# Converting w_in on a timetable during attention, with v loaded from ScalarE's queue and half of the transposed tiles copied by VectorE

## The chip, the cores and the metric

The kernel runs on one core of one Trainium2 chip. A core has five engines that work side by side, each through its own instructions in order: TensorE (PE, matmuls and transposes; PEld is its weight load), VectorE (DVE), ScalarE (ACT), GpSimd (POOL) and SyncE (SP), which here only starts transfers (DMA) between HBM and the on-chip memory. An instruction that waits for a semaphore holds back everything behind it on its engine. The metric is the device time of one execution in microseconds (us); three runs of the kernel before gave a median of 913.17 us (910.35 to 913.26).

## The reference

Three stages follow each other. Inputs are float32 for q, k and v; the five weight matrices are float64 (a float32 array times a NumPy float64 scalar).

```
q, k, v: (4 batches, 8 heads, 576 positions, 64)
scores = q @ k^T / 8
  heads 0-3: row i sees columns i-31..i            ("local")
  heads 4-7: row i sees columns j<=i, j%32 == i%32 ("strided")
attn = softmax(scores) @ v       -> x: 2304 tokens x 512
h = x @ w_in (512 x 2048);  x = (h * cos(h)) @ w_out (2048 x 512)
g = x @ w_gate; val = x @ w_val (512 x 1536 each)
out = (silu(g) * val) @ w_out2 (1536 x 512)
```

## The kernel before

**Three stretches.** Attention comes first, then the first pair of matrices (w_in, w_out) for five blocks of tokens, then the gated pair. Each wide product is made of three float16 matmuls (`mm3`, L502): the float32 number is scaled and split into a high float16 part, written by ScalarE (`hi_part`), and a low part, written by VectorE (`lo_part`). The scale needs the largest magnitude of the whole matrix, so a matrix is read in full before its first product.

**Attention in steps.** One run is one batch with its four local or its four strided heads; there are eight runs, alternating, and each run has three groups (`Duo`), so 24 groups. The loop at L675 goes through steps k = 0 to 29. Step k issues the mask and score matmuls of group k, the row maxima of group k (`tops`, VectorE, then GpSimd), the exponentials of group k-1 (ScalarE), the sums (VectorE) and the normalisation (GpSimd) of group k-2, the transposes of group k-3 (TensorE) and their copies from the matmul memory (`evac`, L442: two per group, both ScalarE), the product with v of group k-4, and the copy of the result of group k-5 into the token array (`put`, ScalarE). A run uses its q and k from step 3i on and its v from step 3i+4 on. Steps 24 to 29 only drain the pipeline; step 25 also issues the first product with w_in (`up1`, L694), in TensorE's queue ahead of the v products of that step.

**Loads.** All loads are issued by SyncE in the order of the program: q and k of a run (`load_qk`, three buffers), v of a run (`load_v`, two buffers of each kind), and raw float64 weights (`load_raw`, L155, 1 MB per pair of tiles, three buffers; the next pair is issued when the conversion of the oldest has been emitted). w_in has eight raw pairs, w_out comes behind it.

**Conversions.** A raw pair of w_in becomes float32 in four pieces (`conv_steps`, L202): g0 on ScalarE waits for the load and makes a first float32 form, g1 on VectorE takes the maxima of the raw pair, g2 and g3 on VectorE add the low bits. These pieces stand in one list (`fill`), with all the work on weights that follows. `pump(share)` is called twice per step: it adds the share to a credit and emits pieces from the list while the credit is above 0, and every piece takes its cost from the credit. `need(key)` emits pieces until the named one is out, whatever the credit says. Before, the whole list stands there from the start, `pump` begins at step KP = 4, and `begin` puts g0 of a pair ahead of g1 to g3 of the pair before it. In the list the scale and split of the first token block stand between w_in's pairs, and behind the pairs come the maximum of w_in, one scan of w_out, w_in's scale, its split into parts, and the other scans of w_out.

**First matrix pair.** Slots of the loop at L894 are one `up1` each (twelve matmuls); from slot HEAD = 16 on, `down1` (the product with w_out) is issued too, which needs w_out's parts tile by tile. SHARE, SHARE2 and HSHARE say how much VectorE work on later weights each slot emits.

## Time and profile before

| | us |
|---|---|
| median of three runs | 913.17 |
| profiled execution, device time | 910.2 |
| its span, first to last instruction | 908.2 |
| PE busy | 859.4 (95%) |
| DVE busy | 599.1 (66%) |
| ACT busy | 489.0 (54%) |
| POOL busy | 179.0 (20%) |
| mean granted TensorE clock | 0.979 of full speed |

The rows stand in a section below. In a row of a timeline the first two numbers are the start and the length in us, then engine, source line, operation, tiles and shapes; the bracket says how long the engine had stood idle and what ended the wait. A busy share is an average over the three stretches, so the attention stretch (up to about 110 us) has to be read by itself.

### The profile page before, as it was taken

The numbers are of one execution on the slowest core, as the hardware profiler recorded it, in microseconds if no ns is written. First come the engines' busy times: TensorE is split into PE (matmuls) and PEld (weight loads), VectorE is DVE, ScalarE is ACT, GpSimd is POOL, SyncE is SP. The second block draws the span as 40 slices with busy tenths as digits, with TensorE's granted clock in tenths as the row PEclk, the third lists the DMA queues.
The fourth block names the chain that finished last, engine by engine and source line by source line (L and its number), as shares of the span: only waits on it lengthen the run. The fifth ranks groups of instructions, "written<-read, shape, count | busy, mean of one in ns | idle before, by whom it ended". The sixth has DMA issues, their size and how long they took to land.

```text
span 908.2 us, 16426 instructions
## 1 busy us (share of the span) xinstructions
PE 859.4 (95%) x6687; PEld 564.6 (62%) x6687; DVE 599.1 (66%) x1038; ACT 489.0 (54%) x942; POOL 179.0 (20%) x202
## 2 busy tenths in 40 slices
PE   8578988998999989999999999999999999999997
PEld 5457744443444434455656677777767777888885
DVE  5358879998578879885778455555644555564544
ACT  4469878864446657554667443443434443444433
POOL 4134404311134546622222100000000000000000
PEclk9689999999999999999999999999999999999999
DMA  9977525257545545553141442424425343544500
GB/s 281 302 257 248 187 114 212 93 186 297 212 183 182 204 151 197 200 209 137 47 174 68 176 163 82 163 109 182 148 97 183 114 156 128 200 183 185 200 1 35
DMA packets 24642, 150.90 MB, mean 166 GB/s; under 512 B 3016, under 2 KB 4296, under 8 KB 11640
## 3 DMA queue, kind: packets, MB, share of 16 engines
q1 hardware_dynamic: 24568, 149.87, 46.3%
q8 instruction: 52, 0.85, 0.4%
q14 instruction: 22, 0.18, 0.1%
HBM read 134.13 MB, written 15.73 MB: 165 GB/s over the span
## 4 chain that ended last, share of the span: by engine, by line
PE 78%; DVE 7%; DMA 6%; ACT 5%; POOL 2%; issue 2%; SPq 0%; POOLq 0%; DVEq 0%; ACTq 0%
PE bank L503 14%; PE bank L504 14%; PE bank L505 14%; PE acc L504 11%; PE acc L505 11%; PE acc L503 11%; DMA raw<-w_in 3%; DMA vs<-v_s 2%; DVE tb L539 1%; PE sc L405 1%; DVE cv L241 1%; PE bank L439 1%; ACT arena L253 1%; DVE arena L256 1%; POOL arena L551 1%
## 5 line engine op out<-in xcount | busy, mean ns | idle before, releaser
L503 PE MATMUL bank<-xs,wi 128*128 128x256 f16 (+3 forms) x744 | 224.9, 302 | 10.9 <-DVE q L134 9.1
L504 PE MATMUL bank<-xs,wi 128*128 128x256 f16 (+3 forms) x744 | 225.0, 302 | 0.0
L505 PE MATMUL bank<-xs,wi 128*128 128x256 f16 (+3 forms) x744 | 224.6, 302 | 0.0
L503 PE MATMUL acc<-arena 128*128 128x512 f16 (+1 forms) x560 | 200.4, 358 | 1.0 <-ACT arena L625 1.0
L504 PE MATMUL acc<-arena 128*128 128x512 f16 (+1 forms) x560 | 200.4, 358 | 0.3 <-DVE arena L626 0.3
L505 PE MATMUL acc<-arena 128*128 128x512 f16 (+1 forms) x560 | 200.4, 358 | 0.0
L551 POOL TENSOR_TENSOR arena<-tb,arena 128x512 f16<-128x512 f32 (+1 forms) x80 | 90.3, 1130 | 248.5 <-ACT arena L550 231.6
L962 DVE TENSOR_TENSOR arena<-bank,cv 128x512 f32<-128x512 f32 (+1 forms) x90 | 57.1, 635 | 117.6 <-PE bank L505 117.6
L505 PEld LDWEIGHTS <-arena 128*128 128x128 f16 x952 | 93.1, 98 | 57.1 <-issue 0.5
L504 PEld LDWEIGHTS <-arena 128*128 128x128 f16 x952 | 93.2, 98 | 53.4 <-issue 1.5
L503 PEld LDWEIGHTS <-arena 128*128 128x128 f16 x952 | 93.2, 98 | 52.6 <-issue 0.6
L504 PEld LDWEIGHTS <-wi 128*128 128x128 f16 x768 | 75.5, 98 | 50.7 <-issue 14.1
L503 PEld LDWEIGHTS <-wi 128*128 128x128 f16 x768 | 75.6, 98 | 43.7 <-issue 6.5
L504 PE MATMUL bank<-xs,arena 128*128 128x256 f16 (+1 forms) x392 | 102.4, 261 | 0.0
L503 PE MATMUL bank<-xs,arena 128*128 128x256 f16 (+1 forms) x392 | 102.4, 261 | 0.0
L505 PE MATMUL bank<-xs,arena 128*128 128x256 f16 (+1 forms) x392 | 102.4, 261 | 0.0
L505 PEld LDWEIGHTS <-wi 128*128 128x128 f16 x768 | 75.5, 98 | 35.4 <-issue 2.4
L625 ACT ACTIVATE arena<-tb 128x512 f16<-128x512 f32 (+1 forms) x60 | 35.2, 587 | 111.0 <-DVE tb L621 111.0
L536 ACT ACTIVATE tb<-bank,quarter,c 128x512 int32<-128x512 f32 (+1 forms) x74 | 53.6, 724 | 47.7 <-PE bank L505 41.8
L614 ACT ACTIVATE tb<-arena,c 128x512 f32<-128x512 f32 (+1 forms) x60 | 40.7, 679 | 66.4 <-DVE arena L962 65.4
L550 ACT ACTIVATE arena<-tb 128x512 f16<-128x512 f32 (+1 forms) x80 | 46.6, 582 | 42.7 <-PE acc L505 38.4
L620 DVE SCALAR_TENSOR_TENSOR tb<-tb,arena 128x512 f32<-128x512 f32 (+1 forms) x60 | 38.0, 634 | 38.9 <-ACT tb L614 38.9
(120 smaller groups left out, 1206.9 us busy)
## 6 DMA issues: line engine op xcount, KB each, us to landing
raw<-w_out SPq DMA_DIRECT2D x28, 1024.0 KB, 4.9
wi<-w SPq DMA_DIRECT2D x16, 1792.0 KB, 7.5
arena<-w SPq DMA_DIRECT2D x14, 1792.0 KB, 7.4
raw<-w_gate SPq DMA_DIRECT2D x12, 1024.0 KB, 4.9
raw<-w_val SPq DMA_DIRECT2D x12, 1024.0 KB, 5.2
w<-arena SPq DMA_DIRECT2D x42, 256.0 KB, 2.1
raw<-w_in SPq DMA_DIRECT2D x8, 1024.0 KB, 20.2
qk<-qk_s SPq DMA_DIRECT2D x4, 1188.0 KB, 7.6
```

The lines of the kernel that those rows point to most:

```text
L241: nc.vector.scalar_tensor_tensor(out=u, in0=box["l"], scalar=29, in1=u, op0=ALU.logical_shift_right, op1=ALU.bitwise_or)
L253: nc.scalar.activation(out=dst, in_=src, func=AF.Copy, scale=s)
L503: nc.tensor.matmul(out=o, lhsT=w[:, 0, c], rhs=x[0], start=first, stop=False, **kw)
L504: nc.tensor.matmul(out=o, lhsT=w[:, 0, c], rhs=x[1], start=False, stop=False, **kw)
L505: nc.tensor.matmul(out=o, lhsT=w[:, 1, c], rhs=x[0], start=False, stop=last, **kw)
L536: nc.scalar.activation(out=c["w"].bitcast(I32), in_=c["ph"], func=AF.Identity, scale=turn[c["blk"]], bias=quarter)
L550: nc.scalar.activation(out=g[:, 0, 0:n], in_=w, func=AF.Copy)
L551: nc.gpsimd.tensor_tensor(out=g[:, 1, 0:n], in0=w, in1=g[:, 0, 0:n], op=ALU.subtract)
L614: nc.scalar.activation(out=t, in_=c["C"][m][:, 0, 0:n], func=AF.Tanh, scale=half[c["blk"]])
L620: nc.vector.scalar_tensor_tensor(out=t, in0=t, scalar=1.0, in1=gate, op0=ALU.add, op1=ALU.mult)
L625: nc.scalar.activation(out=g[:, 0, 0:n], in_=t, func=AF.Copy)
L962: nc.vector.tensor_tensor(out=c["C"][m][:, :, h * right:h * right + h], in0=p, in1=t, op=ALU.add)
```

## The change

Five things are edited. (1) The pairs of w_in leave the common list: pair j is put in at step 4 + 3j (CONV0), g0 to g3 of a pair together; the scale and the split of the first token block are put in at steps 12 and 14; everything behind w_in's pairs is put in at step 25, when the last pair is. `pump` runs from step 0 with share 1.0, and g1 costs 1.2 where it cost 1.6. (2) In `evac` the second of a group's two tiles is copied by VectorE. (3) `load_v` is issued by ScalarE, and the loads of the second run's v and the first raw pair change places. (4) HEAD is 17 where it was 16. (5) SHARE and SHARE2 are 0.95 and 0.75 where they were 0.93 and 0.68.

```diff
--- before.py
+++ after.py
@@ -49,16 +49,16 @@
 
 LAGS = (2, 3, 4, 5)
 WARM = 11
-PUMP, KP, PACE, TAIL = 0.9, 4, 1.6, 1.2
-XSAT = 8
+PUMP, PACE, TAIL, CONV0 = 1.0, 1.2, 1.2, 4
+XSAT = 12
 EARLY, K0 = 1, 1
-HEAD, HSHARE = 16, 0.85
+HEAD, HSHARE = 17, 0.85
 RATE, MINLAG = 0.4, 2
 RAW = 3
 XM = 5
 HOMES, LATE, UNIT = 24, 4, 16
 W7S = 4
-SHARE, SHARE2, SB = 0.93, 0.68, 2
+SHARE, SHARE2, SB = 0.95, 0.75, 2
 
 
 WHERE = [((q, c), (3 + q, c)) if q < 3 else ((6, 0), (6, 256))
@@ -366,11 +366,11 @@
             b, loc = runs[i]
             if loc:
                 v_t[i] = ap.tile([LW, 2, LT, 128], F32, name="vl")
-                nc.sync.dma_start(out=v_t[i], in_=v_l[b])
+                nc.scalar.dma_start(out=v_t[i], in_=v_l[b])
             else:
                 v_t[i] = v_pads[i // 2 % 2]
                 for r in range(2):
-                    nc.sync.dma_start(out=v_t[i][64 * r:64 * r + SW, r], in_=v_s[b, r])
+                    nc.scalar.dma_start(out=v_t[i][64 * r:64 * r + SW, r], in_=v_s[b, r])
 
         def bank():
             return pm.tile([128, 512], F32, name="bank")
@@ -442,8 +442,8 @@
             def evac(self):
                 pt = ap.tile([128, 768], F32, name="pt", bufs=2)
                 self.pt = pt[0:self.rows, 0:2 * self.cols].rearrange("p (u n) -> p u n", u=2)
-                for u in range(2):
-                    nc.scalar.activation(out=self.pt[:, u], in_=self.tp[u], func=AF.Copy)
+                nc.scalar.activation(out=self.pt[:, 0], in_=self.tp[0], func=AF.Copy)
+                nc.vector.tensor_copy(out=self.pt[:, 1], in_=self.tp[1])
 
             def values(self):
                 qn, r = (64, LW) if self.loc else (SW, 64 + SW)
@@ -645,8 +645,8 @@
             nc.sync.dma_start(out=t, in_=a)
         load_qk(1)
         load_v(0)
+        load_v(1)
         load_raw()
-        load_v(1)
         load_qk(2)
         load_raw()
         load_v(2)
@@ -654,17 +654,26 @@
         warm = score_banks()[:, 0]
         for _ in range(WARM):
             nc.tensor.matmul(out=warm, lhsT=ones16, rhs=hot, start=True, stop=True)
-        for j in range(0, M1, 2):
-            chain_later(j)
-            for cost, fn in list(scale_pieces(0, sx)) if j == XSAT else list(split_pieces(0, sx, xs)) if j == XSAT + 2 else ():
-                later(cost, fn)
-        top_later("in")
-        scan_later("out", 0)
-        scale_later("in", TW_IN)
-        split_chain([("in", j, wi) for j in range(M1)], 2)
-        for j in range(1, M1 // 2):
-            scan_later("out", j)
-        top_later("out")
+        due = {CONV0 + 3 * j: [(j,)] for j in range(M1 // 2)}
+        due.setdefault(XSAT, []).append(scale_pieces(0, sx))
+        due.setdefault(XSAT + 2, []).append(split_pieces(0, sx, xs))
+
+        def work_due(k):
+            for what in due.pop(k, ()):
+                if type(what) is tuple:
+                    chain_later(2 * what[0])
+                    begin([])
+                else:
+                    for cost, fn in what:
+                        later(cost, fn)
+            if not due and k == max(XSAT + 2, CONV0 + 3 * (M1 // 2 - 1)):
+                top_later("in")
+                scan_later("out", 0)
+                scale_later("in", TW_IN)
+                split_chain([("in", j, wi) for j in range(M1)], 2)
+                for j in range(1, M1 // 2):
+                    scan_later("out", j)
+                top_later("out")
 
         steps = deque()
 
@@ -677,7 +686,8 @@
                 return gs[k - lag] if 0 <= k - lag < len(gs) else None
 
             i, g = k // 3, k % 3
-            share = 0 if k < KP else PUMP if duo(0) else TAIL
+            share = PUMP if duo(0) else TAIL
+            work_due(k)
             if duo(LAGS[3]):
                 duo(LAGS[3]).put()
             if duo(LAGS[0]):
```

ScalarE's queue around the first two conversions. The steps are 3 to 6; L230 is g0 of a pair, L446 (L445 in the change) the copy of a transposed tile, L419 the exponentials, L467 `put`. Before:

```order
L446 ACTIVATE pt<-bank 96x384 x2
L419 ACTIVATE e_s_97<-sc,mx 128x54 x8
L230 ACTIVATE wi<-raw 128x1024 x2
L467 ACTIVATE xy<-bank 128x2x192
L446 ACTIVATE pt<-bank 96x384 x2
L419 ACTIVATE e_s_98<-sc,mx 128x54 x8
L230 ACTIVATE wi<-raw 128x1024
L467 ACTIVATE xy<-bank 128x2x192
```

With the change:

```order
L373 DMA xs<-v_s 54x1536 x2
L445 ACTIVATE pt<-bank 96x384
L419 ACTIVATE e_s_97<-sc,mx 128x54 x8
L230 ACTIVATE wi<-raw 128x1024
L467 ACTIVATE xy<-bank 128x2x192
L445 ACTIVATE pt<-bank 96x384
L419 ACTIVATE e_s_98<-sc,mx 128x54 x8
L467 ACTIVATE xy<-bank 128x2x192
L445 ACTIVATE pt<-bank 128x256
```

Before, two raw pairs are asked for in step 4 and a third in step 5; now one is asked for in step 4 and none in steps 5 and 6. One L445 per group is left, and loads of v (L373) stand between the copies.

VectorE's queue from step 23 to the first split tile of w_in (the first L256): L233, L237 and L241 are g1, g2 and g3 of the last raw pair, L117 to L127 the maximum of w_in, L176 the scan of w_out, L134 to L111 the scale. Before:

```order
L237 TENSOR_SCALAR wi<-wi 128x1024
L411 TENSOR_REDUCE mx<-sc 128x8
L241 SCALAR_TENSOR_TENSOR wi<-raw,wi 128x1024
L427 TENSOR_REDUCE ls<-e_s_97 128x8
L428 RECIPROCAL ls<-ls 128x8
L117 TENSOR_REDUCE m<-pw_in 128x1
L120 TENSOR_SCALAR a<-m 128x1
L122 SCALAR_TENSOR_TENSOR p<-m,a 128x1
L127 TENSOR_SCALAR tops<-id_72,p 128x128
L411 TENSOR_REDUCE mx<-sc 128x2x3
L176 TENSOR_REDUCE pw_out<-raw 128x2
```

With the change:

```order
L427 TENSOR_REDUCE ls<-e_s_97 128x6
L428 RECIPROCAL ls<-ls 128x6
L233 TENSOR_REDUCE pw_in<-raw 128x2
L237 TENSOR_SCALAR wi<-wi 128x1024
L241 SCALAR_TENSOR_TENSOR wi<-raw,wi 128x1024
L117 TENSOR_REDUCE m<-pw_in 128x1
L120 TENSOR_SCALAR a<-m 128x1
L122 SCALAR_TENSOR_TENSOR p<-m,a 128x1
L127 TENSOR_SCALAR tops<-id_72,p 128x128
L176 TENSOR_REDUCE pw_out<-raw 128x2
L134 TENSOR_REDUCE q<-bank 128x1
L109 RECIPROCAL s_1576<-q 128x1
```

Before, the last pair's g2 and g3 stand in steps 22 and 23 between the maxima of the last groups and the maximum of w_in stands in step 24; now the last pair and all that follows stand behind the sums of the last group, in step 25.

SyncE's queue at the start: L362 loads q and k, L162 a raw pair, L369 and L373 v. Before:

```order
L362 DMA qk<-qk_s 128x2376
L369 DMA vl<-v_l 96x2304
L162 DMA raw<-w_in 128x2048
L373 DMA vs<-v_s 54x1536 x2
L362 DMA qk<-qk_l 128x2368
L162 DMA raw<-w_in 128x2048
L369 DMA vl<-v_l 96x2304
L162 DMA raw<-w_in 128x2048
```

With the change:

```order
L362 DMA qk<-qk_s 128x2376
L162 DMA raw<-w_in 128x2048
L362 DMA qk<-qk_l 128x2368
L162 DMA raw<-w_in 128x2048 x2
L362 DMA qk<-qk_s 128x2376
```

The loads of v are gone from this queue; the first four of them stand at the head of ScalarE's queue, ahead of its first table load.

## Rows read from the trace of the kernel before

**Rows 1.** Page, chain that ended last: shares by line.

```profile
PE bank L503 14%; PE bank L504 14%; PE bank L505 14%; PE acc L504 11%; PE acc L505 11%; PE acc L503 11%; DMA raw<-w_in 3%; DMA vs<-v_s 2%; DVE tb L539 1%; PE sc L405 1%; DVE cv L241 1%; PE bank L439 1%; ACT arena L253 1%; DVE arena L256 1%;
```

**Rows 2.** Waits, 0 to 260 us: waiter, line, releaser: us, times, longest.

```profile
ACT wi L230 <- DMA raw<-w_in: 23.2, 4, 11.2
```

**Rows 3.** Timeline of ScalarE and SyncE: second pair asked for; its load.

```profile
7.25 0.43 SPq L162 DMA_DIRECT2D raw<-w_in  x1
...
31.25 1.14 ACT L230 ACTIVATE wi<-raw 128x1024 f32<-128x1024 f32 x1 [11.21 <-DMA raw<-w_in]
```

**Rows 4.** Windows: stretch, busy by engine, clock, DMA share, GB/s.

```profile
0.00:50.00 50.00, 31.74 (x445) 23.80 (x445) 22.70 (x36) 19.83 (x64) 15.52 (x33) 0.83 0.98 299
...
20.00:30.00 10.00, 2.20 (x52) 1.76 (x49) 2.91 (x5) 0.04 (x1) 1.88 (x2) 0.71 1.00 300
30.00:40.00 10.00, 5.98 (x58) 4.85 (x59) 3.39 (x5) 6.34 (x20) 1.49 (x2) 0.50 1.01 333
...
90.00:100.00 10.00, 9.95 (x208) 8.65 (x204) 9.39 (x15) 9.71 (x31) 5.71 (x6) 1.00 0.42 128
110.00:120.00 10.00, 7.54 (x85) 4.50 (x83) 5.64 (x11) 7.49 (x15) 1.17 (x1) 0.84 0.20 82
```

**Rows 5.** Loads, 0 to 130 us: times issued, KB each, median us to landing.

```profile
raw<-w_in SPq DMA_DIRECT2D x8, 1024.0 KB, 20.2
...
qk<-qk_s SPq DMA_DIRECT2D x4, 1188.0 KB, 7.6
qk<-qk_l SPq DMA_DIRECT2D x4, 1184.0 KB, 19.3
vl<-v_l SPq DMA_DIRECT2D x4, 864.0 KB, 17.2
vs<-v_s SPq DMA_DIRECT2D x4, 324.0 KB
xs<-v_s SPq DMA_DIRECT2D x4, 324.0 KB
```

**Rows 6.** Timeline: TensorE at steps 21, 23, 25 and the first w_in product.

```profile
97.97 1.14 PE L405 MATMUL sc<-qk 64*64 64x54 f32 x32
...
104.26 0.91 PE L405 MATMUL sc<-qk 64*64 64x54 f32 x24
...
109.69 1.11 PE L439 MATMUL bank<-id,e_s 128*128 128x128 f32 x4 [1.92 <-POOL e_s L431]
...
110.60 0.63 PE L503 MATMUL bank<-xs,wi 128*128 128x512 f16 x1
```

**Rows 7.** Lines, 0 to 260 us: shapes, count | busy, mean ns | idle before.

```profile
L446 ACT ACTIVATE pt<-bank 96x384 f32<-96x384 f32 (+1 forms) x48 | 19.0, 459 | 2.5 <-PE bank L439 2.3
L411 DVE TENSOR_REDUCE mx<-sc 128x6 f32<-128x576 f32 (+2 forms) x24 | 15.8, 660 | 14.2 <-PE sc L405 12.6 <-POOL e_l L431 1.4
L233 DVE TENSOR_REDUCE pw_in<-raw 128x2 f32<-128x1024 f32 x8 | 9.5, 1194 | 8.2 <-DMA raw<-w_in 8.2
L241 DVE SCALAR_TENSOR_TENSOR wi<-raw,wi 128x1024 int32<-128x1024 int32 x8 | 9.5, 1193 | 0.0
L427 DVE TENSOR_REDUCE ls<-e_l 128x6 f32<-128x582 f32 x12 | 9.0, 751 | 6.2 <-ACT e_l L419 6.2
L237 DVE TENSOR_SCALAR wi<-wi 128x1024 int32<-128x1024 int32 x8 | 6.0, 746 | 0.9 <-ACT wi L230 0.9
L517 DVE TENSOR_SCALAR xy<-acc,c 128x512 f32<-128x512 f32 x2 | 1.5, 750 | 8.7 <-PE acc L505 8.7
```

**Rows 8.** Timeline of VectorE: maximum of w_in, scan, first split tile.

```profile
105.17 0.84 DVE L122 SCALAR_TENSOR_TENSOR p<-m,a 128x1 int32<-128x1 int32 x1
...
106.62 1.21 DVE L176 TENSOR_REDUCE pw_out<-raw 128x2 f32<-128x1024 f32 x1
```

**Rows 9.** Waits of TensorE, 110 to 340 us.

```profile
PE bank L503 <- DVE q L134: 6.9, 4, 3.5
PE bank L133 <- DVE tops L127: 2.5, 1, 2.5
```

## Prediction

> **What bounds the kernel now.** I read the chain of waits first. By line its long shares are the matmuls of the two later stretches, and behind them stand two loads, raw<-w_in with 3% and vs<-v_s with 2% [rows 1]: the only part of the chain that is not arithmetic lies in attention. The list of waits puts a number on it: ScalarE stood 23.2 us, in four waits, in front of g0 of a raw pair of w_in [rows 2]. The timeline shows the worst: the pair's load was issued at 7.25 and g0 began at 31.25, after 11.21 us of idling [rows 3]; the order shows that this g0 stood in step 4, in front of `put`, the copies and the exponentials of step 5, so attention stopped with it. In that stretch TensorE was busy 2.20 of 10 us and the granted clock fell to 0.71, then 0.50 [rows 4]. Last I read the windows for what is short there: from 0 to 50 us the DMA engines were busy for 0.98 of the time at 299 GB/s, between 90 and 100 only 0.42, and there TensorE was busy 9.95 of 10 us, VectorE 9.39 and ScalarE 9.71 [rows 4]. So early attention is short of bytes and spends it on weights that nobody needs yet, and late attention has every engine full.
>
> **The stall goes; what is late next.** With a pair at steps 4, 7, 10 the waits of 23.2 us lose their cause, but the bytes remain. Up to step 21 all q and k, all v but the last, and seven of eight raw pairs must have landed; the last v lies among them in the queues. That is 4 x (1188 + 1184) + 4 x 864 + 8 x 324 + 7 x 1024 = 22,704 KB [rows 5], 23.25 MB, and at 299 GB/s [rows 4] 78 us; with the start and the landing I put the scores of step 21 at 80. Before they began at 97.97 [rows 6]. Bounds: at the best 10 us of the trace, 333 GB/s [rows 4], 70 us of loading, and then the engines decide (below); at the slow end the engines' pace is worse than before.
>
> The order of the loads follows the need: the first three v no longer stand in SyncE's queue, where q and k of the third run and the raw pairs were behind them. ScalarE pays for it. It issues twelve loads, and four of them stand ahead of its first table load; the waits among them are for loads that the first scores need as well. From step 6 on a load of v waits for the v products of the same step, and the next thing on ScalarE, `put` of the next step, waits for the same products, so only a g0 or exponentials queued behind would feel it. Two queues share the start: q and k of the first run compete with v, some 2 us on the first scores, which the byte count above already holds.
>
> With one queue the DMA engines were busy for 0.98 of the first 50 us [rows 4], so I give the second queue no bandwidth. The Trainium skill says the same in "DMA: Bandwidth & Descriptors", section "Issuing engines are not separate DMA queues": transfers started by different engines run on the same DMA engines, interleave, and save only issue time. By that rule the 78 us stand; if ScalarE's queue had bandwidth of its own, SyncE's would carry 16,656 KB, an estimated 57 us, and the engines would decide alone.
>
> **The engines' pace.** Steps 21 to 23 took (104.26 - 97.97) / 2 = 3.15 us each [rows 6]. ScalarE loses one copy per group, 24 x 0.459 = 11 us [rows 7], and gains twelve load issues. VectorE gains 24 copies. The trace has no such copy on VectorE: the nearest row from the same memory is 750 ns for 512 columns (L517), the lower end is ScalarE's 459 ns for 384 or 256; scaled by columns L517 gives 0.56 and 0.38, and I take 0.47 [rows 7]. Per three steps VectorE then has 3 x (0.66 maxima + about 0.85 sums and reciprocal + 0.47) = 5.9, and one pair 1.19 + 0.75 + 1.19 = 3.1 [rows 7], together 9.0 or 3.0 per step, beside TensorE's 3.15. That fits on average. But the pair now falls into one step: about 5.1 us of VectorE in a step of 3.15, which then has two steps to catch up. Between 0 and 0.6 us per step; I take nearly 0, since the bytes hold the steps back anyway.
>
> **Step 25.** From step 21's scores to the transposes of step 25 it was 109.69 - 97.97 = 11.7 us [rows 6]; 80 + 11.7 = 91.7. There the cost of the timetable comes due: the last pair and all behind it stand in step 25, ahead of the first product. On VectorE in a row: sums 0.75, the pair 3.1 [rows 7], the maximum of w_in 106.62 - 105.17 = 1.45, and from the scan to the first product 110.60 - 106.62 = 4.0 with other work between [rows 6, 8]; 9.3 at most, and without that other work 8.4. The first product with w_in comes at about 100 where it came at 110.6: a gain of 10.6 us. TensorE has little to do in these 8 us, since the v products of step 25 stand behind the first product.
>
> **After attention.** Both matrix stretches keep TensorE busy nearly throughout, so the gain should carry to the end, less three things. The forced pieces leave a debt in the credit, so scans and conversions of w_out are emitted later by several slots, and in the order the maximum, scale and first split of w_out now stand directly before the first `down1`, where three slots lay between. One more slot (HEAD) covers part. Priced by the same chain, 4.0 us, against 2.5 that TensorE waited for such a maximum before [rows 8, 9]: I take +2, from -2.5 to +6. The idle gap in step 25 drops the clock: it was 0.84 from 110 to 120 after a short gap [rows 4]; +1, from 0 to 3. SHARE and SHARE2 emit later weights sooner; the last blocks have room on VectorE, so 0, and if VectorE fills there the waits for its scale (6.9 us in four [rows 9]) grow by some of themselves, 0 to 4.
>
> **Sum.** -10.6 + 2 + 1 = -7.6. The profiled execution took 910.2 (span 908.2 and 2.0 around it), so 902.6. It was the fastest of the times seen, 3 below the median of 913.2; for a median I add half of that: 904.
>
> **Rivals.** *Loads faster than I think.* At 333 GB/s step 21 could come at 72; by pace, a step 6 at 26 us and fifteen steps of 3.15 give 73. The first product comes near 93, 7 earlier: 897. For it: 333 was reached while little else ran [rows 4]. Against: the mean of 299 holds for 50 us. *VectorE takes the place of the loads.* Bursts of 5.1 us delay sums and maxima, and the exponentials and transposes behind them; 0.6 us in each of some 16 steps is 10 us and eats the gain: 911. For it: VectorE stood at 9.39 of 10 before it had copies [rows 4]. Against: ScalarE, the fuller one, is relieved. The change failing to do what it says, raw pairs still landing too late, has the same price and belongs here. *Slower.* The debt makes w_out's tiles come just in time: if each of the sixteen `down1` of the first block waits for one low part, 0.75 us as a pass over 512 columns takes (L517) [rows 7], that is 12 us, and 5 more for the first: -10.6 + 17 + 1 gives 918. It decides once TensorE's waits there pass some 13 us. Against: in those slots TensorE has two products of work for each conversion, and such waits were small before [rows 9].
>
> **Chances.** Forecast 0.56, with a range of its own from 898 to 909.5; faster loads 0.12; VectorE 0.20; late weights 0.12. A measurement of this kernel tells about 0.3%, 2.7 us, from no change, so faster means below 910.4. Faster: 0.56 + 0.12 + 0.05 of VectorE's = 0.73; within: 0.13 + 0.02 = 0.15; slower: 0.02 + 0.10 = 0.12. The range, 895 to 914, reaches over most of faster loads and of VectorE's case and leaves out the slow end.
>
> **What would show it.** ScalarE's wait for raw w_in under 5 us in all; a DMA share near 1.0 until about 75 us; the scores of step 21 near 80 and the first w_in product near 100, with a gap of about 8 us on TensorE before it that ends on VectorE or ScalarE; a wait of a few us before the first `down1`. Wrong would be a first product after 106 (the pace), before 95 (the loads), or one near 100 with the end not earlier (the weights).

## The result: 1.3% slower, and the profile after

The changed kernel took 923.9 us (median of 4 runs, 922.06 to 924.41); the kernel before, on the same chip, 912.47. The ratio is 1.0133, with a 95% interval from 1.0109 to 1.0157. Ratios here and below are estimates from the single executions and not the quotient of the two medians, which is 1.0125 here. Forecast were 904 us, in a range from 895 to 914: the sign was wrong, and the time lies outside the range. The profiled execution took 924.41, its span is 922.4 us. One execution of b_dense, a run below, took 2283.4 us and is left out of that run's figures.

I cut both spans at five marks that stand in both programs: the first row maxima (L411, step 0), the maxima of steps 9 and 23, the first product with w_in (L503), and the first store of the output (issued by SyncE).

| stretch | before, us | after, us | difference |
|---|---|---|---|
| start to maxima of step 0 | 8.61 | 17.32 | +8.7 |
| to maxima of step 9 | 47.61 | 35.90 | -11.7 |
| to maxima of step 23 | 49.99 | 55.49 | +5.5 |
| to the first w_in product | 4.39 | 9.95 | +5.6 |
| to the first output store | 499.96 | 506.15 | +6.2 |
| to the end | 297.6 | 297.6 | 0.0 |

The gain that the change was forecast to bring is there, 11.7 us between steps 0 and 9, and four stretches eat 26.

**The raw waits are gone.** The list of waits of the changed kernel, 0 to 260 us (waiter, line, releaser: us, times, longest), has in the place of [rows 2]:

```profile
ACT L419 <- DMA qk<-qk_l: 12.0, 1, 12.0
...
ACT wi L230 <- DMA raw<-w_in: 0.8, 1, 0.8
```

23.2 us became 0.8, but a wait of 12.0 us stands at the start. It is that of ScalarE's first table load behind its own loads of v; it costs nothing by itself, since the first exponentials begin at 18.41, after 5.1 us of waiting for the maxima. The chain of the page has other loads in the place of raw<-w_in and vs<-v_s [rows 1]:

```profile
PE bank L503 14%; PE bank L504 14%; PE bank L505 14%; PE acc L504 10%; PE acc L503 10%; PE acc L505 10%; DMA qk<-qk_s 3%; DVE arena L256 2%; DMA ml<-mask_l 1%; DVE tb L539 1%; PE sc L405 1%; ACT arena L253 1%; ACT e_s L419 1%; DVE tb L546 1%; DVE cv L241 1%
```

The new entry is ml<-mask_l, the 96 KB mask that the first score matmul needs. The timeline of TensorE (start, length, instruction, and in the bracket the idle time before it and its releaser) and the list of load issues of the first 20 us (KB each, median us to landing) show what it did:

```profile
14.15 0.40 PE L394 MATMUL sc<-ml,id 128*128 128x288 bf16 x1 [8.02 <-DMA ml<-mask_l]
...
15.09 2.19 PE L405 MATMUL sc<-qk 64*64 64x96 f32 x24
```

```profile
ml<-mask_l SPq DMA_DIRECT2D x1, 96.0 KB, 12.5
...
ms<-mask_s SPq DMA_DIRECT2D x1, 54.0 KB, 12.2
```

In the kernel before the two masks landed 4.9 and 4.6 us after their issue, and the first scores began at 7.35 (its list of issues, then its timeline):

```profile
ml<-mask_l SPq DMA_DIRECT2D x1, 96.0 KB, 4.9
```

```profile
7.35 1.21 PE L405 MATMUL sc<-qk 64*64 64x96 f32 x24
```

SyncE issued the four constants between 1.2 and 2.8 us in both kernels, so they were not sent later: they took longer. Of the 8.7 us at step 0, 7.7 are the later start of the first scores (15.09 against 7.35); the other 1.0 is that they took 2.19 us where they took 1.21. TensorE had stood idle for 8.02 us, and its granted clock was 0.50 (1.2 GHz) from 14 to 18 us, where it was 1.00 (2.4 GHz) from 7 to 11 before.

The delay goes on in SyncE's queue. By its list of waits (0 to 60 us) the next load there, a raw pair, waited for a constant to land, and the keys (q and k) that step 9 needs reuse the buffer of the first run, whose last scores end at 21.70. They were asked for at 21.74 (before: 13.96), and step 9's scores waited for them (SyncE's waits, then TensorE's timeline):

```profile
SPq L162 <- DMA id<-eye: 10.3, 1, 10.3
```

```profile
51.14 1.96 PE L405 MATMUL sc<-qk 64*64 64x54 f32 x32 [2.23 <-DMA qk<-qk_s]
```

**From step 9 on the loads no longer hold the steps, and VectorE is the fullest engine.** The windows (length, busy time of PE, PEld, DVE, ACT, POOL, then granted clock, DMA share, GB/s), beside [rows 4]:

```profile
60.00:70.00 10.00, 8.62 (x175) 7.29 (x172) 9.49 (x25) 7.13 (x26) 3.17 (x7) 1.00 0.93 255
70.00:80.00 10.00, 8.53 (x185) 7.45 (x184) 9.81 (x16) 8.30 (x26) 3.54 (x4) 1.00 0.91 262
...
90.00:100.00 10.00, 8.96 (x164) 7.77 (x162) 8.51 (x15) 7.19 (x20) 2.94 (x6) 0.95 0.40 151
...
110.00:120.00 10.00, 3.39 (x36) 1.71 (x34) 7.56 (x18) 4.30 (x11) 1.65 (x2) 0.74 0.53 192
```

VectorE is at 9.5 and 9.8 of 10 from 60 to 80 us, while the loads leave the DMA engines partly idle; from 80 to 110 us it has 8.2 to 8.5, and no engine is full. Step 21's scores began at 100.02 (before 97.97 [rows 6]). In the last row TensorE has 3.39 us of work in 10: that is step 25, and its timeline and VectorE's beside it read like this:

```profile
111.11 0.66 PE L439 MATMUL bank<-id,e_s 128*128 128x128 f32 x4
...
116.20 0.29 PE L133 MATMUL bank<-tops,ones 128*128 128x128 bf16 x1 [4.43 <-DVE tops L127]
...
118.66 0.61 PE L503 MATMUL bank<-xs,wi 128*128 128x512 f16 x1 [2.17 <-ACT wi L253]
```

```profile
112.35 1.18 DVE L233 TENSOR_REDUCE pw_in<-raw 128x2 f32<-128x1024 f32 x1
113.45 0.68 DVE L237 TENSOR_SCALAR wi<-wi 128x1024 int32<-128x1024 int32 x1
114.17 1.22 DVE L241 SCALAR_TENSOR_TENSOR wi<-raw,wi 128x1024 int32<-128x1024 int32 x1
...
115.89 0.25 DVE L127 TENSOR_SCALAR tops<-id,p 128x128 bf16<-128x128 bf16 x1
116.06 1.21 DVE L176 TENSOR_REDUCE pw_out<-raw 128x2 f32<-128x1024 f32 x1
117.19 0.28 DVE L134 TENSOR_REDUCE q<-bank 128x1 f32<-128x128 f32 x1
```

The last pair's three passes, the maximum, a scan of w_out and the scale stand in a row between the last transposes and the first product: 118.66 - 111.11 = 7.55 us.

**After attention** the first `down1` waits, and later so do two products and a maximum that come behind VectorE:

```profile
183.08 0.61 PE L503 MATMUL acc<-arena 128*128 128x512 f16 x1 [2.51 <-ACT arena L253]
...
355.47 0.38 PE L503 MATMUL bank<-xs,wi 128*128 128x512 f16 x1 [1.53 <-DVE tb L546]
...
400.56 0.22 PE L133 MATMUL bank<-tops,ones 128*128 128x128 bf16 x1 [2.00 <-DVE tb L546]
403.87 0.48 PE L503 MATMUL bank<-xs,wi 128*128 128x384 f16 x1 [3.09 <-DVE q L134]
```

From the first product to the first store TensorE is idle for 20.8 us (before 17.3) and busy for 485.3 (before 482.7).

### The profile page after: what moved, and what is told of

Its sections match the earlier page's. It is cut to its first block, busy times and chain, and to the rows that moved or that the text cites. A ratio compares the mean times of both kernels' runs of the same rounds, so it can differ in the third digit from the quotient of the medians.

```text
span 922.4 us, 16429 instructions
## 1 busy us (share of the span) xinstructions
PE 863.8 (94%) x6687; PEld 566.3 (61%) x6687; DVE 608.9 (66%) x1062; ACT 483.5 (52%) x918; POOL 170.8 (19%) x202
## 4 chain that ended last, share of the span: by engine, by line
PE 74%; DVE 11%; ACT 5%; DMA 5%; issue 3%; POOL 2%; SPq 0%; ACTq 0%; POOLq 0%; DVEq 0%
PE bank L503 14%; PE bank L504 14%; PE bank L505 14%; PE acc L504 10%; PE acc L503 10%; PE acc L505 10%; DMA qk<-qk_s 3%; DVE arena L256 2%; DMA ml<-mask_l 1%; DVE tb L539 1%; PE sc L405 1%; ACT arena L253 1%; ACT e_s L419 1%; DVE tb L546 1%; DVE cv L241 1%
## 5 line engine op out<-in xcount | busy, mean ns | idle before, releaser
L503 PE MATMUL bank<-xs,wi 128*128 128x256 f16 (+3 forms) x744 | 224.7, 302 | 15.2 <-DVE q L134 9.8
L503 PE MATMUL acc<-arena 128*128 128x512 f16 (+1 forms) x560 | 201.4, 360 | 3.5 <-ACT arena L253 2.5
L503 PEld LDWEIGHTS <-arena 128*128 128x128 f16 x952 | 93.4, 98 | 55.2 <-ACT arena L253 2.8
L503 PEld LDWEIGHTS <-wi 128*128 128x128 f16 x768 | 75.6, 98 | 47.2 <-issue 4.4
L503 PE MATMUL bank<-xs,arena 128*128 128x256 f16 (+1 forms) x392 | 102.4, 261 | 0.0
```

The costliest lines, as they stand in the source:

```text
L503: nc.tensor.matmul(out=o, lhsT=w[:, 0, c], rhs=x[0], start=first, stop=False, **kw)
```

## The experiments

Theory: the loss has four places, each with its own cause: v on a second queue (start), the timetable (pace and step 25), VectorE's copies (pace), SHARE2 and its companions (after attention). Rivals stand with each run. All ratios are to the kernel before on the same chip; 0.001 is 0.9 us. The marks are those of the table above, in us from the start of the span, of one profiled execution each. How far such marks scatter is seen in o_share: its program differs from the kernel before only behind attention, and yet its first product comes 2.4 us earlier. The diffs show the lines that matter; those of the u runs, x_const and f_two are against the changed kernel, the others against the kernel before or the run named.

| run | median, us | ratio (95%) | step 0 | step 23 | product | first store |
|---|---|---|---|---|---|---|
| before | | | 8.61 | 106.21 | 110.60 | 610.56 |
| changed | 923.9 | 1.0133 (1.0109-1.0157) | 17.32 | 108.71 | 118.66 | 624.81 |
| u_v | 914.6 | 1.0034 (1.0016-1.0051) | 8.68 | 97.58 | 107.52 | 612.99 |
| u_evac | 921.81 | 1.0127 (1.0100-1.0153) | 16.50 | 106.48 | 117.12 | 621.50 |
| u_share | 919.11 | 1.0088 (1.0062-1.0114) | 16.56 | 108.04 | 117.99 | 620.70 |
| u_time | 920.18 | 1.0101 (1.0081-1.0120) | 16.72 | 107.30 | 111.35 | 620.48 |
| o_time | 911.31 | 1.0006 (0.9990-1.0023) | 8.32 | 98.58 | 109.22 | 612.02 |
| o_v | 908.72 | 0.9985 (0.9968-1.0003) | 17.30 | 104.67 | 108.85 | 609.61 |
| o_share | 917.02 | 1.0071 (1.0043-1.0099) | 8.25 | 104.20 | 108.18 | 617.05 |
| x_const | 922.17 | 1.0124 (1.0100-1.0147) | 12.93 | 106.09 | 116.03 | 622.12 |
| b_dense | 914.73 | 1.0051 (1.0033-1.0070) | 8.29 | 101.70 | 105.16 | 613.85 |
| b_dense2 | 915.54 | 1.0055 (1.0026-1.0084) | 8.23 | 104.14 | 109.06 | 615.54 |
| b_dense_late | 920.37 | 1.0118 (1.0080-1.0156) | 8.32 | 109.16 | 112.61 | 622.06 |
| b_late | 910.95 | 1.0005 (0.9987-1.0024) | 8.23 | 108.11 | 112.51 | 613.19 |
| c_s2 | 914.45 | 1.0044 (1.0030-1.0059) | 8.22 | 98.60 | 109.25 | 614.58 |
| c_sh | 910.2 | 0.9994 (0.9978-1.0010) | 8.31 | 97.96 | 108.94 | 609.83 |
| c_head | 910.91 | 1.0005 (0.9988-1.0021) | 8.47 | 98.38 | 109.37 | 610.58 |
| f_two | 912.15 | 1.0024 (1.0007-1.0041) | 8.74 | 99.56 | 109.51 | 613.59 |
| f_mid | 904.06 | 0.9933 (0.9911-0.9955) | 8.33 | 100.20 | 110.84 | 609.36 |
| f_v | 908.54 | 0.9979 (0.9962-0.9996) | 16.32 | 104.56 | 108.84 | 609.06 |

### One part undone in the changed kernel

**u_v**, v back on SyncE:

```diff
-                nc.scalar.dma_start(out=v_t[i], in_=v_l[b])
+                nc.sync.dma_start(out=v_t[i], in_=v_l[b])
-        load_v(1)
         load_raw()
+        load_v(1)
```

> The changed kernel with v put back on SyncE's queue, in its old place of the load order; the timetable, the VectorE copy and the two shares stay. Theory (the first scores start at 15.1 us instead of 7.4 us because v on a second queue shares the DMA engines with the three small constants, and the 7.7 us are carried to the end): constants land after 4 to 5 us, first scores within 9 us, first w_in product at 111 instead of 118.7, time 916 us (914 to 918). Rival (the late start is made up by waits for raw pairs and keys that come back when the cores' work starts earlier): product still at 117 or later, time 922 to 925 us.

Measured 914.6; the ratio falls by 0.0099, 9.0 us. The same rows as above, of this run:

```profile
ml<-mask_l SPq DMA_DIRECT2D x1, 96.0 KB, 4.9
```

The constants are early again and the 8.6 us at step 0 reach the end whole: step 9's keys are asked for at 13.64 and its scores begin at 41.06, 10.1 us earlier, and the product comes 11.1 us earlier. The theory holds for the price: v's queue, with the order of loads that goes with it, is three quarters of the loss of 0.0133. Whether the late constants alone make it is tried in x_const.

**u_evac**, both copies on ScalarE:

```diff
-                nc.scalar.activation(out=self.pt[:, 0], in_=self.tp[0], func=AF.Copy)
-                nc.vector.tensor_copy(out=self.pt[:, 1], in_=self.tp[1])
+                for u in range(2):
+                    nc.scalar.activation(out=self.pt[:, u], in_=self.tp[u], func=AF.Copy)
```

> The changed kernel with both transposed tiles copied on ScalarE again; timetable, v on ScalarE's queue and the shares stay. Theory (the VectorE copies, about 48 of 0.4 to 0.5 us, sit on the engine that sets the pace from step 9 on, 3.96 us a step): pace of steps 9 to 23 falls to about 3.7 us, first product 3 to 4 us earlier, time 919 us (917 to 921). Rival (the burst of a whole pair in one step sets that pace, not the copies; ScalarE becomes as full as VectorE was): pace stays at 3.9 to 4.0, time 923 to 926 us.

Measured 921.81, a fall of 0.0006 with intervals of 0.0025 on either side: no effect that can be told. The pace of steps 9 to 23 went from 3.96 to (106.48 - 52.38) / 14 = 3.86 us. The copies are not what sets it; the rival stands on that point. (The expectation counted 48 VectorE copies; there are 24.)

**u_share**, the old figures for the work after attention:

```diff
-HEAD, HSHARE = 17, 0.85
+HEAD, HSHARE = 16, 0.85
-SHARE, SHARE2, SB = 0.95, 0.75, 2
+SHARE, SHARE2, SB = 0.93, 0.68, 2
```

> The changed kernel with the old figures for the weights' pace after attention (17, 0.95 and 0.75 back to 16, 0.93 and 0.68). Theory (the some 6 us lost after the attention part come from weights that are converted later because the timetable leaves a debt of work, not from these figures): time 924 us, within 2 us of the changed kernel, and the waits before the first down products stay. Rival (the figures put too much conversion work beside the first block): time 918 us, and the waits of 2.5 to 2.9 us at 156 and 183 us go.

Measured 919.11, a fall of 0.0045 (4.1 us), between the two. The waits at 156 and 180 us stayed (2.86 and 2.19 us), so the rival's reason fails; but those at 355 and 400 us went (0.38 us is left at 395). I had looked for the figures' price in the wrong place.

**u_time**, the old list and pump:

```diff
-PUMP, PACE, TAIL, CONV0 = 1.0, 1.2, 1.2, 4
-XSAT = 12
+PUMP, KP, PACE, TAIL = 0.9, 4, 1.6, 1.2
+XSAT = 8
-        due = {CONV0 + 3 * j: [(j,)] for j in range(M1 // 2)}
+        for j in range(0, M1, 2):
+            chain_later(j)
```

> The changed kernel with the old work list and pump of the conversion (no timetable); v on ScalarE's queue, the VectorE copy and the shares stay. Theory (the timetable takes away some 12 us of raw waits but gives back some 7 in the chain before the first product and some 6 in late weights, so that it is worth little in itself): time 919 to 924 us, ScalarE waits over 10 us for raw pairs again, and the gap before the first product is under 2 us. Rival 1 (the timetable is the gain of the change and v's queue alone its loss): time over 928 us. Rival 2 (the timetable is itself the loss): time under 915 us.

Measured 920.18: as the theory has it, the timetable is worth little in itself. The product came at 111.35, 7 us earlier than in the changed kernel, although the start was as late: the old list's step-25 gap is 4 us, not 10. It is lost again later: 509 us from the product to the first store, against 506 in the changed kernel and 500 before. Its pace from step 9 to 23 is 3.59 us, with the copies on VectorE, against 3.96 with the timetable.

The four ratios fall by 0.0099, 0.0006, 0.0045 and 0.0032. Their sum is 0.0182, more than the whole loss of 0.0133: the prices of the parts do not add.

### One part alone on the kernel before

**o_time**, the timetable alone:

```diff
-PUMP, KP, PACE, TAIL = 0.9, 4, 1.6, 1.2
+PUMP, PACE, TAIL, CONV0 = 1.0, 1.2, 1.2, 4
-        for j in range(0, M1, 2):
-            chain_later(j)
+        due = {CONV0 + 3 * j: [(j,)] for j in range(M1 // 2)}
...
+            work_due(k)
```

> The kernel before with the timetable of the conversion alone (pairs at fixed steps, statistics of xs at step 12, the piece costs that belong to it); v on SyncE's queue, copies on ScalarE, old shares. Theory (the losses of the changed kernel add up: start 9, shares 4 to 5, copies under 1, so that the timetable is near nothing: its 12 us of raw waits are paid back by a slower pace from step 9 on, by the chain before the first product and by the converted weights that come late): 910 us (908 to 912), first product near 107, and 3 to 4 us lost again between there and the end. Rival 1 (the timetable is the gain; copies or shares hid it): 905 us or less. Rival 2 (it is itself a loss): 914 us or more.

Measured 911.31, no difference: the theory. The marks show where it went. At step 23 it is 7.6 us ahead, at the product 1.4, and from product to first store it loses 2.8 more. Its pace from step 9 to 23 is (98.58 - 44.87) / 14 = 3.84 us against 3.57 before, without one copy on VectorE: 3.7 us over fourteen steps. All eleven profiles with a pair at every third step have 3.84 to 4.06; those with the old list have 3.43 to 3.61, but for b_late with 3.95. So the timetable itself slows the steps. The difference is clearest in steps 17 to 23, where the DMA engines are no bound. Windows of the kernel before, and of this one:

```profile
87.19:106.21 19.02, 18.75 (x375) 16.41 (x376) 16.88 (x31) 18.54 (x62) 10.80 (x13) 1.00 0.38 122
```

```profile
77.00:98.58 21.58, 18.58 (x374) 16.24 (x374) 15.89 (x26) 18.25 (x62) 8.05 (x12) 1.00 0.54 162
```

The same TensorE work takes 2.6 us longer, and VectorE has less to do, not more. Before, at most one pass of a pair stands between a step's maxima (L411) and its sum (L427); from 95.92 to 97.73 that is 1.8 us (VectorE, kernel before):

```profile
95.92 0.76 DVE L411 TENSOR_REDUCE mx<-sc 128x6 f32<-128x576 f32 x1 [0.51 <-PE sc L405]
96.59 1.22 DVE L241 SCALAR_TENSOR_TENSOR wi<-raw,wi 128x1024 int32<-128x1024 int32 x1
97.73 0.75 DVE L427 TENSOR_REDUCE ls<-e_l 128x6 f32<-128x582 f32 x1
```

Here two passes stand there, with a wait for g0 of the same pair ahead of them: 3.3 us, from the maxima at 83.19 to the sum at 86.44 (VectorE, then TensorE, of this run):

```profile
84.57 0.69 DVE L237 TENSOR_SCALAR wi<-wi 128x1024 int32<-128x1024 int32 x1 [0.63 <-ACT wi L230]
85.30 1.22 DVE L241 SCALAR_TENSOR_TENSOR wi<-raw,wi 128x1024 int32<-128x1024 int32 x1
86.44 0.75 DVE L427 TENSOR_REDUCE ls<-e_l 128x6 f32<-128x582 f32 x1
...
87.34 0.73 DVE L411 TENSOR_REDUCE mx<-sc 128x6 f32<-128x576 f32 x1
...
91.20 0.61 DVE L411 TENSOR_REDUCE mx<-sc 128x8 f32<-128x432 f32 x1 [2.24 <-PE sc L405]
```

```profile
88.78 0.86 PE L439 MATMUL bank<-id,e_l 128*96 128x128 f32 x6 [1.32 <-POOL e_l L431]
```

The sum comes late, with it GpSimd's normalisation and TensorE's transposes; the scores behind them are late, and then VectorE itself idles 2.24 us. The chain of work that ended last goes through this burst (start and length in us), g0 on ScalarE, then VectorE's two passes and the sum:

```profile
83.50 1.06 ACT wi L230
84.57 0.71 DVE wi L237
85.30 1.22 DVE wi L241
86.53 0.68 DVE ls L427
```

It does so again at 94.89; in the kernel before no piece of a pair of w_in lies on that chain between 77 and 106 us. No run spreads the pieces of a pair over the steps of the timetable, so that this would win the pace back is not shown. And two waits appear late, in the gated pair (TensorE's timeline):

```profile
518.75 0.27 PE L503 MATMUL bank<-xs,wi 128*128 128x256 f16 x1 [1.38 <-DVE arena L972]
527.49 0.27 PE L503 MATMUL bank<-xs,wi 128*128 128x256 f16 x1 [3.33 <-ACT cv L968]
```

There VectorE and ScalarE still convert the last weights (L237, L241, L253 lie between, in their timelines). Work that the timetable postpones comes due here.

**o_v**, v's queue alone, and **f_v**, the same kernel measured again:

```diff
-                nc.sync.dma_start(out=v_t[i], in_=v_l[b])
+                nc.scalar.dma_start(out=v_t[i], in_=v_l[b])
-        load_raw()
         load_v(1)
+        load_raw()
```

> The kernel before with v's loads alone moved to ScalarE's queue. First scores near 15 us instead of 7.4 us under either theory. Theory (under the old list the kernel then waits for its raw pairs until after 35 us anyway, so that a late start costs little there; it costs 9 us only where the timetable has taken those waits away): first product within 2 us of before, time 911 to 914 us. Rival (the late start is carried to the end whatever the list): first product near 118, time 918 to 920 us.

> The kernel before with v's loads alone on ScalarE's queue, once more in five rounds. Theory (the late start is hidden by the wait for the first raw pairs, and the keys no longer queue behind v, worth 1 to 2 us): 908.5 to 910 us, ratio 0.998 to 0.9995. Rival (the first figure was scatter): 910 to 912 us, ratio 0.9995 to 1.001.

Measured 908.72 and 908.54; in the second the interval, 0.9962 to 0.9996, excludes 1. The start is as late as in the changed kernel (17.30), step 9 is level with the kernel before (56.67 and 56.22), and the product comes 1.75 us earlier, which is within the scatter of single profiles. In the list of waits ScalarE now stands before raw pairs for:

```profile
ACT L419 <- DMA qk<-qk_l: 12.0, 1, 12.0
ACT wi L230 <- DMA raw<-w_in: 10.7, 2, 10.4
```

10.7 instead of 23.2 [rows 2]: the same bytes have to land before the first pairs, and waiting for constants or for pairs is the same time. So the same edit costs 9 us with the timetable and gains 2 without it.

**o_share**, the three figures alone (the diff of u_share the other way round):

```diff
-HEAD, HSHARE = 16, 0.85
+HEAD, HSHARE = 17, 0.85
-SHARE, SHARE2, SB = 0.93, 0.68, 2
+SHARE, SHARE2, SB = 0.95, 0.75, 2
```

> The kernel before with the new shares of the conversion work after attention alone (17, 0.95 and 0.75). Theory (the shares start conversion work of the later blocks earlier than VectorE can take it, and TensorE then waits for its maxima and casts between 300 and 400 us; they cost the same 4 to 5 us with the old list as with the timetable): 915 to 917 us, with new waits of 1.5 us and more on VectorE between 300 and 420 us. Rival 1 (they cost only where weights come late from the timetable): 910 to 912.5 us. Rival 2 (they and not the rest explain why the changed kernel with the old list lost 9 us): 918 us or more.

Measured 917.02, 6.5 us slower: the theory. The wait that it named is there (TensorE's timeline), and the kernel before has none over 0.8 us between 330 and 460 us:

```profile
384.37 0.32 PE L503 MATMUL bank<-xs,wi 128*128 128x384 f16 x1 [3.09 <-DVE tb L546]
```

From the product to the first store TensorE is idle for 24.4 us, against 17.3 before.

### The start

**x_const**, the four constants on ScalarE's queue too, ahead of v:

```diff
-            nc.sync.dma_start(out=t, in_=a)
+            nc.scalar.dma_start(out=t, in_=a)
```

> The changed kernel with the four small constant loads (246 KB) moved to ScalarE's queue too, ahead of v; qk stays first on SyncE's. Theory (the constants are late because they stand behind 1.2 MB of qk on their own queue while the other queue's v takes half of the DMA engines; ahead of v they land about as early as before, and v comes later but is not wanted at once): constants land within 6 us, first scores at 8 to 10 us, time 915 to 917 us. Rival (two queues at once are slow for small loads in whatever order, or qk itself comes late instead): first scores at 12 us or later, time 919 us or more.

Constants landed after 8.6 us and the first scores began at 10.70, 4.4 us earlier than in the changed kernel; the time was 922.17, the rival's. Being first on their queue doesn't restore the 4.9 us: q and k of two runs, 2.4 MB on the other queue, are issued at 0.73 and 1.17, and v follows. At step 9, 1.1 us of the 4.4 were left: its keys were asked for at 17.34, 4.4 us earlier, and landed only after 32.7 us instead of 29.4; TensorE waited for them:

```profile
50.02 1.96 PE L405 MATMUL sc<-qk 64*64 64x54 f32 x32 [6.72 <-DMA qk<-qk_s]
```

At the product 2.6 us were left, and the ratio is only 0.0009 lower, inside both intervals. So half of the late start given back is not half of the 9 us: beside the constants, keys come late as well when v has a queue of its own, and how the 9 us divide between the two stays open.

### Can the timetable be repaired?

**b_dense** and **b_dense2**: o_time with the pairs at other steps, the last before step 25.

```diff
-        due = {CONV0 + 3 * j: [(j,)] for j in range(M1 // 2)}
+        PAIRS = (4, 7, 10, 13, 15, 17, 19, 21)
+        due = {PAIRS[j]: [(j,)] for j in range(M1 // 2)}
```

> The timetable alone (v on SyncE, ScalarE copies, old shares) with the eight pairs at steps 4, 7, 10, 13, 15, 17, 19, 21 instead of every third step to 25. Theory (with pairs at every third step, attention is some 7 us ahead at step 23 and loses it in step 25, where the last pair's maximum, the common scale and the first cast stand between the last transposes and the first product): the gap before the first product shrinks from 10.6 us after the maxima of step 23 to under 6, product at 103 to 105, time 905 us (903 to 908). Rival (VectorE's work is only moved, and the steps 13 to 21 become longer by what step 25 saves): product at 107 to 109, time 909 to 912 us.

> As the run before it, with the pairs two steps apart from the second on: 4, 7, 9, 11, 13, 15, 17, 19. Theory (the raw pairs and the keys share the DMA engines, which are full until about 50 us; two pairs in each three steps ask for some 4 MB a run of steps, over 13 us at 300 GB/s, so that waits for raw pairs come back while VectorE gets its work done sooner): waits for raw pairs of 3 us or more in steps 7 to 13, product within 1 us of the run before, time 904 to 908 us. Rival 1 (bandwidth is there): product 2 us earlier than in the run before. Rival 2 (the engines are blocked by the early pairs, step 9 to 13 wait as in the old list): time 910 us or more.

Both missed: 914.73 and 915.54. The step-25 gap closes as foreseen (101.70 to 105.16 is 3.5 us, product 4.1 us earlier than in o_time), but product to first store takes 508.7 us where it took 502.8, with waits for VectorE of 1.9, 2.3, 2.3 and 4.7 us at 163, 206, 213 and 329 us, where o_time has 1.3 at 214 and 2.4 at 324; TensorE's idle time between these marks is 24.4 us against 17.8. What TensorE gains before the product it waits for behind it. In b_dense2 the keys are late (4.8 us at 80 us) and the product is where it was.

**b_dense_late** and **b_late**: only the last five v loads on ScalarE's queue, on b_dense and on the kernel before.

```diff
+            queue = nc.sync if i < 3 else nc.scalar
-                nc.sync.dma_start(out=v_t[i], in_=v_l[b])
+                queue.dma_start(out=v_t[i], in_=v_l[b])
```

> The dense timetable (4, 7, 10, 13, 15, 17, 19, 21) with the first three v loads on SyncE in the old order and the later five on ScalarE's queue. Theory (the second queue costs only where its big loads meet the small constants at the start; later it is free, and SyncE's queue no longer holds a v behind a raw load that waits for its buffer): first scores at 7 to 7.5 us, time within 2 us of the dense timetable alone or up to 2 us less, 903 to 907 us. Rival (two queues at once slow each other's keys in the middle too): new waits for keys over 3 us, time 909 us or more.

> The kernel before with only the later five v loads on ScalarE's queue, the first three on SyncE's. Theory (the later v on their own queue are free and v's move alone already gave 1.7 us with a start 7 us later, because the old list's wait for raw pairs hides the start): first scores at 7 to 7.5 us, time 907 to 911 us, the waits for raw pairs over 15 us still. Rival (the early move is what helped the old list, as it let the keys come first): 911 to 913 us.

920.37 and 910.95. The start is early, as expected (8.32 and 8.23), yet the first is 6 us slower than b_dense: TensorE waited 6.3 and 4.6 us for keys, the rival's mark, where b_dense waited 4.3 once. So in this timetable the later loads of v delay keys when they have their own queue; on the kernel before the same edit makes no difference that can be told. That would leave the early v as the source of o_v's gain, but this was not tried apart, and the intervals of b_late and f_v overlap.

### The three figures

Each alone on o_time; **c_s2**, **c_sh** and **c_head**:

```diff
-SHARE, SHARE2, SB = 0.93, 0.68, 2
+SHARE, SHARE2, SB = 0.93, 0.75, 2
```

> The timetable alone (v on SyncE, ScalarE copies) with the second share alone raised, 0.68 to 0.75; head 16 and share 0.93 as before. Theory (the timetable is 4.6 us ahead of the kernel before at 456 us and loses it in waits of 1.4 and 3.3 us at 518 and 527 us, where the last conversion work is still on VectorE and ScalarE; a higher second share takes it earlier): those two waits go, nothing new at 355 and 400 us, time 905 to 908 us. Rival (the second share itself brings the waits at 355 and 400 us): waits of 1.5 us or more there, time 911 to 916 us.

```diff
-SHARE, SHARE2, SB = 0.93, 0.68, 2
+SHARE, SHARE2, SB = 0.95, 0.68, 2
```

> The timetable alone with the first share alone raised, 0.93 to 0.95. Theory (the first share governs the blocks until the third and puts the conversion ahead of the TensorE-bound stretch; a change of 2% moves single pieces only): time within 2 us of the timetable alone, 909 to 913 us, the waits at 518 and 527 us at most partly gone. Rival (it brings the waits at 355 and 400 us): those waits of 1.5 us or more, time 914 us or more.

```diff
-HEAD, HSHARE = 16, 0.85
+HEAD, HSHARE = 17, 0.85
```

> The timetable alone with the head alone longer, 16 to 17 slots before the first down product. Theory (one more slot of the first block before the downs shifts all later pairs of up and down work and thereby which conversion pieces stand ahead of the maxima and casts that TensorE waits for at 355 and 400 us): waits of 1.5 us or more at 355 or 400 us, time 914 to 918 us. Rival (the longer head only gives the late weights more time): no such waits, the wait of 2.2 us before the first down product smaller, time 908 to 911 us.

914.45, 910.2 and 910.91: SHARE2 is the one that costs (0.0038 over o_time, 3.5 us); HEAD and SHARE alone make no difference that can be told. TensorE's timeline in c_s2:

```profile
326.14 0.59 PE L503 MATMUL bank<-xs,wi 128*128 128x512 f16 x1 [4.49 <-DVE q L134]
...
392.65 0.22 PE L133 MATMUL bank<-tops,ones 128*128 128x128 bf16 x1 [1.56 <-DVE tb L546]
394.17 0.48 PE L503 MATMUL bank<-xs,wi 128*128 128x384 f16 x1 [1.30 <-DVE q L134]
...
526.48 0.27 PE L503 MATMUL bank<-xs,wi 128*128 128x256 f16 x1 [0.48 <-DVE arena L972]
```

The waits of o_time at 518 and 527 us are gone or 0.48 us, and 2.9 us appear at 393 with 2.1 more at 326 (2.37 in o_time): the share moves the waits.

**f_two**, the changed kernel with u_v's edit and SHARE2 alone back:

```diff
-SHARE, SHARE2, SB = 0.95, 0.75, 2
+SHARE, SHARE2, SB = 0.95, 0.68, 2
```

> The changed kernel with two things undone: v back on SyncE's queue and the second share back at 0.68. The timetable, the VectorE copies, head 17 and share 0.95 stay. Theory (v's queue, some 9 us, and the second share, 4 to 6 us, are the whole loss, and the rest is worth nothing): 910 us (908 to 912), no difference from the kernel before that can be measured. Rival 1 (the rest has a loss of its own): 913 us or more. Rival 2 (the rest is a gain once freed): 907 us or less.

912.15, at the theory's edge; the interval, 1.0007 to 1.0041, keeps up to 3.7 us of loss of its own for what is left in it, the VectorE copies against c_sh and c_head. And SHARE2 brought only 0.0010 here (0.9 us): the waits of 1.4 and 3.3 us at 520 and 529 us came back. The prices of the parts do not simply add.

**f_mid**, o_time with HEAD 17, SHARE 0.95 and a second share between:

```diff
-HEAD, HSHARE = 16, 0.85
+HEAD, HSHARE = 17, 0.85
-SHARE, SHARE2, SB = 0.93, 0.68, 2
+SHARE, SHARE2, SB = 0.95, 0.70, 2
```

> The timetable with ScalarE copies, v on SyncE, head 17, share 0.95 and a second share between the two, 0.70. Theory (conversion work is conserved: a share too low leaves waits at 520 us, one too high makes them at 326 and 393 us, and a value between can at best save the smaller of them): 907 to 911 us, one of the two groups of waits still there. Rival (between them both groups vanish): 904 to 906 us.

904.06, a ratio of 0.9933 to the kernel before and, by 0.9933 / 1.0133, 2.0% under the changed one: nearer to the rival. The waits at 393 and around 520 us are gone or under 0.5 us; at 325 us 1.64 are left, where o_time has 2.37:

```profile
324.70 0.38 PE L503 MATMUL bank<-xs,wi 128*128 128x512 f16 x1 [1.64 <-DVE q L134]
...
390.08 0.32 PE L503 MATMUL bank<-xs,wi 128*128 128x384 f16 x1 [0.38 <-DVE q L134]
...
521.26 0.27 PE L503 MATMUL bank<-xs,wi 128*128 128x256 f16 x1 [0.48 <-DVE arena L972]
```

That explains little of the 904 us. The profiled execution was the longest of the ten (909.21; the other nine took 902.8 to 908.13), and it is no shorter than c_sh's (909.55), which has 4.14 us of waiting at 324 and 2.5 around 520: from the product to the first store it gains 2.4 us, but its product comes at 110.84, 1.9 later. What differs in the other nine is their granted clock: 0.981 to 0.987, against 0.977 in the profiled one and 0.976 to 0.983 in 27 executions of the kernel before, of which the shortest (905.99) had 0.983 and the longest (914.76) 0.976. So the gain in the median is measured, but how much of it is waits and how much is clock no profile here can tell.

## Why the prediction was wrong

**The raw waits: right.** 23.2 us became 0.8, and steps 0 to 9 took 11.7 us less.

**Where the 21.8 us lie.** The forecast for the profiled execution was 902.6, and it took 924.4. At step 21's scores, forecast for 80, 20.0 of these 21.8 were there: 11.1 go with v's queue (88.90 in u_v), and 8.9 are left without it. From there to the product it was 1.4 us shorter than forecast, and behind the product 3.2 longer.

**The start: the step that failed most.** I priced two queues by bytes, "some 2 us on the first scores". It was 7.7 (15.09 against 7.35), and u_v shows 9.0 us at the end for v's queue as a whole. The fault was to count the first scores' bytes as one sum. They need a set: 1.2 MB of keys and 246 KB of constants, and a small load's time to land is not its bytes over the rate: 96 KB took 12.5 us beside v on the other queue, 4.9 with v behind them. And I did not follow the delay on, to the loads behind the constants on SyncE's queue and to the keys of step 9, which still held that step in every profile with the timetable (2.2 us of waiting in the changed kernel, 4.5 in u_v, 6.7 in x_const). I had written that the waits "are for loads that the first scores need as well" and drew no price from it. The Trainium skill's rule that I used ("DMA: Bandwidth & Descriptors", "Issuing engines are not separate DMA queues") was borne out for bandwidth, 273 GB/s over the first 50 us against 299 before, and says nothing of this order. The same page, "Queues, rings and completion order", states that a load's completion mark is written only behind every earlier write of that DMA engine, across its queues. That fits the constants' late landing; no run here shows the mechanism.

**Bytes as the bound: right up to step 9, wrong behind it, and with them the engines' pace.** Step 21's scores were put at 80 us. They came at 100.02, and with v back on SyncE still at 88.90, in a kernel whose DMA share had fallen to 0.77 between 70 and 80 while VectorE stood at 9.85 between 60 and 70 (windows of u_v):

```profile
60.00:70.00 10.00, 7.65 (x157) 6.60 (x157) 9.85 (x17) 8.14 (x24) 3.54 (x4) 1.00 0.93 224
70.00:80.00 10.00, 7.10 (x155) 6.17 (x152) 9.19 (x17) 7.28 (x26) 5.78 (x5) 1.00 0.77 241
```

The engines hold the steps. I took their pace from the last two steps, 3.15 us; the kernel before has 3.57 as the mean of steps 9 to 23, with work on the first token block in some of them, the timetable 3.84, with copies 3.9. "Between 0 and 0.6 us per step; I take nearly 0" was the wrong choice in the range: 0.27 by o_time, 3.7 us. I had added up VectorE's work against TensorE's, found that it fits, and left out that each step's sum stands in a chain through three engines. My rival of VectorE had the mechanism, bursts that delay the sums and the transposes behind them, and a price of 0.6 us a step. I also summed it wrongly: 10 us on a forecast of 904 are 914 and not 911.

**Step 25: right.** 8.4 us forecast between the last transposes and the product, 7.55 measured. The old list has 0.91 there [rows 6], and the forecast of 100 held that difference; its gain of 10.6 us failed because the 18 us forecast at step 21 did not come. Of the 7.6 us that o_time is ahead at step 23, 6.2 go here.

**After attention: the first wait right, the rest mis-sized.** +2 before the first `down1`: the wait for w_out's maximum is there as before (2.85 us, before 2.51), and 2.51 before the product came on top, +2.9 in all. SHARE and SHARE2 at "0, ... 0 to 4": 4.1 by u_share, 3.5 by c_s2 for SHARE2 alone; I had granted the last blocks room on VectorE, but the wait is in the blocks between, behind maxima that TensorE asks for at 326, 393 and 400 us. The clock, +1, does not show where I put it: in the 25 us from the first product on it was 0.94, and 0.88 before. Over the whole stretch to the first store TensorE's busy time is 2.7 us longer; how much of that is clock I could not separate.

**The slower rival** had the right sign for a wrong reason: no train of sixteen small waits in the first block, but one late start, a slower pace and a handful of single waits. And the sum assumed that a gain in attention is carried to the end: b_dense, 5.4 us ahead at the product and 3.3 behind at the first store, shows that it isn't.

## What to carry to other kernels

Before a load is moved to a second queue, list what the first instruction needs and which of it is small: its landing is what the second queue delayed here, and the next keys' with it, and whether that costs depends on whether another wait hides it (o_v gained 2 us where the same edit cost 9). A pace for a stage is read as a mean over all its steps, with the work still in them, not from the last two. And where conversion work is postponed, look for the place where it comes due, and tune the share that spreads it with the timetable, one figure at a time: with the timetable, second shares of 0.68, 0.70 (with HEAD 17 and SHARE 0.95) and 0.75 were 910 to 911, 904 and 914 us.

## What the runs showed that I had not expected

The share of busy DMA engines says little of the bytes moved: over the first 13 us it was 0.89 in the kernel before and in the changed one alike, at 288 and 224 GB/s; x_const, with two queues as well, had 0.89 and 294. f_mid differs from c_sh by one slot of HEAD and 0.02 of SHARE2, and its ratio is 0.0061 lower (5.6 us). Its profile has 2.8 us less idle time of TensorE between the product and the first store and is no shorter as a whole; the nine executions that are shorter had a higher granted clock, and why just this setting has it I can't say from the profiles.
